# Reordered loads and prefix products at the start, output halves in turn at the end, in a fused Mamba-2 and SiLU-MLP kernel on one Trainium2 core

## The chip, the cores and the metric

The kernel runs on one core of a Trainium2 chip. The metric is device time in microseconds (us) of one execution; lower is better. Within the core five engines work side by side, each through its own instructions in order: PE (TensorE, matrix products into PSUM), DVE (VectorE), ACT (ScalarE), POOL (GpSimd) and SP (SyncE), which here only issues DMAs.

## The reference

The first half is a state-space scan over 4 batches, 8 heads and 768 steps in chunks; the second takes its output, 3072 rows of 256, through two dense layers with a SiLU between them.

```python
def _attn_ref(x, a, B, C):          # x (4,8,768,32), a (4,8,768), B and C (4,8,768,16)
    log_a = np.log(np.clip(a, 1e-06, 1.0))
    ...
        cum = np.cumsum(la, axis=-1)
        L = np.exp(cum[:, :, :, None] - cum[:, :, None, :]) * causal
        M = np.einsum('bhin,bhjn->bhij', Cc, Bc) * L
        y_intra = np.einsum('bhij,bhjd->bhid', M, xc)
        y_inter = np.einsum('bhin,bhnd->bhid', Cc, state) * np.exp(cum)[:, :, :, None]
        y[:, :, sl] = y_intra + y_inter
        ...
        state = decay_full * state + np.sum(Bx, axis=2)

def _moe_ref(x, w_in, w_out):       # x (3072,256), w_in (256,2048), w_out (2048,256)
    h = x @ w_in
    return (h * (1.0 / (1.0 + np.exp(-h)))) @ w_out
```

The weights come in 64-bit floats, so the kernel first turns their bits into 32-bit floats by itself.

## The kernel before

**Units and pairs.** The 3072 rows are 12 units of 256 steps (three for each batch); two units make a pair of 512 rows. The scan half makes a unit's output `XF[u]`; the dense half multiplies it by 16 tiles of the weights, numbered 0 to 15: 0 to 7 are `w_in`, 8 to 15 `w_out`, 512 KB each. Pair 0 (units 0 and 1) goes through the plain products `f_s1(u, j)` (unit u, weight j, 8 matmuls, L508) and `f_s2(j)` (the steps "m0" to "m7", L521). Pairs 1 to 5 go through split operands (a high part, a low part, a correction): `s1_d`, `s1_h`, `s2`, `s2_d` (L536, L544, L576 and L577, L590), 16 steps for each pair.

**A unit's scan.** `load_pa` brings the coefficients a in prefix order (tile pz), `load_ab` in another order (ab), `load_n` and `load_t` B and C (bn, tbc), `load_x` x (xt). DVE clips (`f_P0`, only units 0 and 1) and scans the coefficients (`f_P`, L328), and `f_C` (L391) multiplies the scan with C into cw. `f_T` or `f_TP` turn B and C; `f_TP` uses TensorE and leaves C in PSUM, in one of only two halves (pool `ps_h`) that the products hp of `f_s1` use too. `f_Ek` and `f_E1` are the decay scans E; `f_B`, `f_D0`, `f_G`, `f_S`, `f_SM`, `f_M` prepare states and masked products; `f_Y` (L459, L468) makes the unit's output in PSUM and `f_X` copies it out. In the text forms, "2:PTC" means these steps for unit 2, with "1", "2" for the two decay scans, "D" for `f_G` and `f_D0`, "A" for the loads of pa, bn and ab, "L" for all loads.

**A weight.** `load_w(n)` loads it raw (six buffers, "r11" in the text form); ACT takes it apart in `w_size(n)` ("s6"), DVE in three steps in `w_bits(n)` ("b5"), and POOL ends it with an add (L207). Then `w_h`, `w_l`, `w_d` make the split forms.

**What sets the order.** The schedule is written by hand: each engine runs its instructions in the order in which the code calls them. Nearly all loads go through SP's queue. The coefficients of units 2 to 11 are clipped on the chip and written back to two DRAM tiles, `a_in` and `a_zero` (`f_A2`, L262 to L269), from which `load_pa` and `load_ab` read. At L255 a small DMA, the mark, reads a piece of raw weight 3, so that SP goes on to weight 5 only when that has landed. After each `f_s1` ACT applies the SiLU (gT, L511) and so frees the PSUM half; whatever ACT has ahead of gT, `w_size` among it, holds that half.

**The end.** In the last two steps `s2` adds the last products to both output halves m = 0, 1, `s2_d` the corrections, `f_sum2` (L598) scales these on ACT, and `f_end` (L622) combines them on DVE, transposes (L633) and stores (L635) on the queues of SP and ACT.

Of the kernel before, what the change touches and what calls it, by code (L numbers as in the profile page):

```python
# [33 lines left out]
def kernel(  # L34
# [47 lines left out]

    sc.tile([128, 40], FP32, name="pad")
# [40 lines left out]
    def load_t(u, i, q):  # L124
        b, t0 = at(u)
        if u == 0:
            tbc[u] = block("tbc0").rearrange("p (i e r n) -> p i e r n", i=2, e=2, r=8)
        elif u not in tbc:
            tbc[u] = loads.tile([128, 2, 2, 8, N], FP32, name="tbc")
        src = (B, C)[i]  # L130
        if u == 0:
            for g in range(4):
                q.dma_start(out=tbc[u][32 * g:32 * g + 32, i],
                            in_=src[b, 2 * g:2 * g + 2, t0:t0 + UT].rearrange("e (t r) n -> t e r n", r=8))
# [39 lines left out]
    def two(t):  # L174
        return t.rearrange("p (k f) -> p k f", k=2)

    def load_w(n, q):
        j = n % 8
        src = wi[:, :, j * WF:(j + 1) * WF] if n < 8 else wo[:, 2 * j:2 * j + 2]
        if src.dtype == FP32:  # L180
            w32[n] = block("w32")
            q.dma_start(out=two(w32[n]), in_=src)
            return
        t = raw[n] = quad.tile([128, 2, WF, 2], U32, name="raw", tag="quad")
        q.dma_start(out=t.rearrange("p k f two -> p k (f two)"), in_=src.bitcast(U32))  # L185
# [47 lines left out]
    nc.sync.dma_start(out=ach[A0:A1], in_=bass.AP(tensor=a.tensor, offset=a.offset, ap=[[Q, NC0], [S, H], [1, Q]]))  # L233
    pa01 = block("pa01")
    pz = const.tile([128, 4, Q + 1], FP32, name="pz")
    one = const.tile([128, 4, Q + 1], FP32, name="one")
    load_t(0, 1, nc.sync)
    load_n(0, 0, nc.scalar)
    nc.sync.dma_start(out=pa01, in_=bass.AP(tensor=a.tensor, offset=a.offset, ap=[[S, H], [0, N], [1, 2 * UT]]))
    load_x(0, nc.sync)  # L240
    for n in range(3):
        load_w(n, nc.sync)
# [3 lines left out]

    acl, acz = (block(n).rearrange("p (h t) -> p h t", t=Q) for n in ("acl", "acz"))
# [4 lines left out]
    mark = const.tile([1, RAW - 5], U32, name="mark")  # L252
    for n in range(3, RAW):
        if n > 4:
            nc.sync.dma_start(out=mark[:, n - 5:n - 4], in_=raw[n - 2][0:1, 0, 0, 0:1])  # L255
        load_w(n, nc.sync)

# [4 lines left out]
    def f_A2():  # L262

        r = slice(0, NC0 * batch)
        nc.vector.tensor_scalar(out=acl[r], in0=acl[r], scalar1=1.0, scalar2=1e-6, op0=ALU.min, op1=ALU.max)
        nc.vector.tensor_copy(out=acz[r], in_=acl[r])
        nc.vector.memset(acz[r, :, 0:1], 0.0)
        nc.sync.dma_start(out=a_in[:, :, 1:].rearrange("h c t -> c h t"), in_=acl[r])
# [32 lines left out]
    f_A()  # L301
    ident = const.tile([128, 128], FP32, name="ident")
    nc.vector.memset(ident, 0.0)
    nc.gpsimd.affine_select(out=ident, in_=ident, pattern=[[-1, 128]], compare_op=ALU.not_equal,
                            fill=1.0, base=0, channel_multiplier=1)

    diag = const.tile([128, H, Q], FP32, name="diag")
    nc.vector.tensor_copy(out=diag, in_=diag1.to_broadcast([128, H, Q]))
    hm = const.tile([128, H], FP32, name="hm")
# [11 lines left out]

    def f_P0(u):
        src = pa01[:, UT * u:UT * u + UT].rearrange("p (c t) -> p c t", t=Q)
        nc.vector.tensor_scalar(out=pz[:, :, 1:], in0=src, scalar1=1.0, scalar2=1e-6, op0=ALU.min, op1=ALU.max)

    def f_P1(u):
        PFX[u] = sc2.tile([128, 4, Q + 1], FP32, name="pfx")
        nc.vector.tensor_tensor_scan(out=PFX[u].rearrange("p c t -> p (c t)"),  # L328
                                     data0=pz.rearrange("p c t -> p (c t)"),
                                     data1=one.rearrange("p c t -> p (c t)"), initial=0.0,  # L330
                                     op0=ALU.mult, op1=ALU.add)

    def f_P(u):
        if u < 2:
            f_P0(u)
        f_P1(u)

# [50 lines left out]

    def f_C(u):
        CW[u] = sc.tile([128, UT], FP32, name="cw")  # L390
        nc.vector.tensor_tensor(out=CW[u].rearrange("p (c t) -> p c t", t=Q),  # L391
                             in0=CT.pop(u).rearrange("p (c t) -> p c t", t=Q), in1=PFX[u][:, :, 1:], op=ALU.mult)
# [173 lines left out]

    def s2(s):
# [5 lines left out]
        gh, gl = GH.pop(s), GL.pop(s)  # L573
        for m in range(2):
# [90 lines left out]
    f_Y(0)  # L665
# [11 lines left out]
    f_B(1)  # L677
    w_bits(2, 2)
    f_P(1)
    f_C(1)  # L680
    f_G(1)
    f_D0(1)
# [6 lines left out]
    f_A2()  # L689
    for n in range(6, 9):  # L690
        load_w(n, nc.sync)
    load_bcx(2)
    w_bits(3, 2)
# [4 lines left out]
    w_bits(4)  # L698
    load_pa(2, nc.sync)
    load_ab(2, nc.sync)  # L700
    load_w(10, nc.sync)
# [66 lines left out]
    for text in ("m0 3:D 4:L 3:SsM 2:h h1 l1 2:l 2:d d0 b13 s14", "m1 3:Y 3:h h2 l2 d1 b14 s15", "m2 3:l 3:d d2 b15 h3 l3",  # L768
                 "m3 p0 d3 h4 l4 4:T", "m4 h8 l8 d4 h5 l5 d8", "m5 d5 h9 l9 d9"):
        todo(text)  # L770
# [14 lines left out]
    def step(s):  # L785
# [94 lines left out]
```

## Time and profile before

| what | us |
|---|---|
| median of 3 runs (337.47 to 338.9) | 338.38 |
| the profiled execution, its own time | 339.9 |
| its span, first to last instruction | 338.0 |
| PE busy in the span | 322.8 (96%) |
| DVE busy | 252.4 (75%) |
| ACT busy | 218.6 (65%) |
| POOL busy | 69.1 (20%) |
| chain that ended last: PE | 85% |
| the same: issue on SP's queue | 8% |

The chain of work that ended last is followed back from the last instruction. It is TensorE's from 42.96 us to 330 us, and before that mostly SP's queue issuing loads and the landings that it waits for. Shares of busy time are means over the span. The start, up to about 50 us, has other limits than the long middle, so it is to be read from the timeline and from windows cut to it. In a timeline row the columns are start, duration, engine, line, operation and, in brackets, the engine's idle time before it and what ended that. In a row of windows they are the stretch, its length, the busy time of PE, PE's weight loads, DVE, ACT and POOL with their numbers of instructions, the granted TensorE clock, the share of the DMA engines, and GB/s. In a row of waits they are engine, line, what it waited for, the sum in us, how often, and the longest. A DMA's row on SP's queue is its issue and not its transfer.

### The profile page before, as it was taken

The page shows a single profiled execution, that of the slowest core. Times are in us where ns is not written, and L with a number is a line of the kernel's source. Part 1 is how long each engine was busy: PE and PEld are TensorE (multiplying, and loading weights), DVE is VectorE, ACT ScalarE, POOL GpSimd, SP SyncE. Part 2 cuts the span into 40 slices and gives each one's busy share as a digit, 9 for nine tenths or more (in the row PEclk, how much of TensorE's full clock was granted, in tenths as well). Part 3 has the DMA queues.
Part 4 walks back from the last instruction along what each step waited for, and adds up shares of the span by engine and source line. Part 5 has one row for each costly group of instructions (what it writes and reads, how often), then busy time and mean ns, then how long its engine had stood idle before and what let it go on. Part 6 is the DMA issues. An engine that isn't in the chain of part 4 may idle for free.

```text
span 338.0 us, 7790 instructions
## 1 busy us (share of the span) xinstructions
PE 322.8 (96%) x3145; PEld 256.4 (76%) x3146; DVE 252.4 (75%) x420; ACT 218.6 (65%) x417; POOL 69.1 (20%) x66
## 2 busy tenths in 40 slices
PE   8879599999999999999999999999999999999992
PEld 4558478888878778778788778788778788888881
DVE  7998558997677888996965996865996854674443
ACT  3656535956478898767666666767667756666651
POOL 3226313257001222231202230202240202000000
PEclk9999969999999999999999999999999999999998
DMA  6968878795674584154330154420343000020003
GB/s 127 224 211 211 191 185 206 222 170 108 114 150 67 101 157 89 46 112 75 71 78 0 50 107 85 101 40 0 66 104 52 2 2 0 0 49 17 0 2 62
DMA packets 97290, 30.87 MB, mean 91 GB/s; under 512 B 82230, under 2 KB 88374, under 8 KB 97254
## 3 DMA queue, kind: packets, MB, share of 16 engines
q1 hardware_dynamic: 90758, 25.78, 34.1%
q0 software_dynamic: 2304, 4.20, 7.2%
q10 hardware_dynamic: 4192, 0.39, 0.9%
q8 instruction: 25, 0.41, 0.5%
q14 instruction: 11, 0.09, 0.1%
HBM read 22.82 MB, written 3.34 MB: 77 GB/s over the span
## 4 chain that ended last, share of the span: by engine, by line
PE 85%; SPq 8%; DMA 4%; DVE 1%; issue 1%; ACT 0%; DVEq 0%; ACTq 0%
PE hp L544 23%; PE b L590 11%; PE hp L536 11%; PE oa L576 11%; PE oa L577 11%; PE oa L521 8%; PE hp L508 4%; SPq L122 4%; DMA raw<-in_moe_w_in_dram 3%; PE gy L468 2%; PE gy L419 2%; PE gy L459 2%; DMA pz<-a_in 1%; PE gy L407 1%; SPq L185 1%; SPq L145 1%
## 5 line engine op out<-in xcount | busy, mean ns | idle before, releaser
L538 ACT ACTIVATE hp<-hp 128x512 f32<-128x512 f32 x80 | 46.6, 583 | 72.1 <-PE hp L536 72.0
L558 DVE TENSOR_TENSOR gl<-g,gh 128x512 fp32r<-128x512 f32 x62 | 42.7, 689 | 52.2 <-ACT gh L554 49.1
L544 PE MATMUL hp<-xh,wh 128*128 128x512 f32 x160 | 65.2, 407 | 0.0
L562 DVE SCALAR_TENSOR_TENSOR gd<-gh,g 128x512 fp32r<-128x512 f32 x80 | 59.5, 747 | 5.2 <-ACT gh L554 5.2
L544 PE MATMUL hp<-xl,wl 128*128 128x512 f32 x160 | 62.6, 391 | 0.0
L576 PE MATMUL oa<-gh,wh 128*128 128x512 f32 x160 | 62.5, 391 | 0.0
L577 PE MATMUL oa<-gl,wl 128*128 128x512 f32 x160 | 62.4, 390 | 0.0
L558 POOL TENSOR_TENSOR gl<-g,gh 128x512 fp32r<-128x512 f32 x18 | 29.2, 1623 | 121.9 <-ACT gh L554 121.9
L554 ACT ACTIVATE gh<-g 128x512 fp32r<-128x512 f32 x80 | 50.5, 632 | 2.8
L536 PE MATMUL hp<-xd,wd 128*128 128x512 f32 x160 | 49.5, 391 | 0.0
L552 ACT ACTIVATE g<-hp 128x512 f32<-128x512 f32 x80 | 47.5, 593 | 0.5 <-PE hp L544 0.5
L590 PE MATMUL b<-gd,wd 128*128 128x512 f32 x160 | 44.4, 390 | 0.0
L508 PE MATMUL hp<-xf,w 128*128 128x256 f32 x128 | 32.8, 411 | 5.1 <-DVE cw L391 3.3
L544 PEld LDWEIGHTS hp<-xh,wh 128*128 128x128 f32 x160 | 30.0, 188 | 9.1 <-ACT hp L538 2.5
L536 PEld LDWEIGHTS hp<-xd,wd 128*128 128x128 f32 x160 | 30.0, 188 | 6.7
L576 PEld LDWEIGHTS oa<-gh,wh 128*128 128x128 f32 x160 | 30.0, 188 | 6.4
L590 PEld LDWEIGHTS b<-gd,wd 128*128 128x128 f32 x160 | 30.0, 188 | 6.5 <-DVE o L616 0.3
L577 PEld LDWEIGHTS oa<-gl,wl 128*128 128x128 f32 x160 | 30.0, 188 | 6.3
L508 PEld LDWEIGHTS hp<-xf,w 128*128 128x128 f32 x128 | 25.5, 205 | 11.3 <-issue 3.6
L544 PEld LDWEIGHTS hp<-xl,wl 128*128 128x128 f32 x160 | 30.1, 188 | 5.2
L207 POOL TENSOR_TENSOR w<-wu,wv 128x512 uint32<-128x512 uint32 (+1 forms) x20 | 23.3, 1174 | 45.6 <-DVE wv L202 41.7
L521 PE MATMUL oa<-gT,w 128*128 128x256 f32 x128 | 29.0, 381 | 0.0
(81 smaller groups left out, 375.2 us busy)
## 6 DMA issues: line engine op xcount, KB each, us to landing
ab<-a_zero SPq DMA_DIRECT2D x40, 128.0 KB
raw<-in_moe_w_in_dram SPq DMA_DIRECT2D x8, 512.0 KB
raw<-in_moe_w_out_dram SPq DMA_DIRECT2D x8, 512.0 KB
wl<-w POOLq DMA_DIRECT2D x16, 256.0 KB, 4.2
xt<-in_x_dram SPq DMA_DIRECT2D x24, 128.0 KB
out_dram<-ot SPq DMA_DIRECT2D x44, 64.0 KB
bn<-in_B_dram SPq DMA_DIRECT2D x22, 64.0 KB
tbc<-in_C_dram SPq DMA_DIRECT2D x22, 64.0 KB
```

The costliest lines, as they stand in the source:

```text
L508: nc.tensor.matmul(out=hp[:, i], lhsT=two(w32[j])[:, kc, 128 * i:128 * i + 128], rhs=two(XF[u])[:, kc], start=(kc == 0), stop=(kc == KC - 1))
L521: nc.tensor.matmul(out=OA[0][m][:, UT * u:UT * u + UT], lhsT=two(w32[8 + j])[:, i, 128 * m:128 * m + 128], rhs=two(GT[u, j])[:, i], start= ...
L536: nc.tensor.matmul(out=HP[s], lhsT=two(WD[f // 2])[:, kc, 128 * (f % 2):128 * (f % 2) + 128], rhs=XD[P][:, kc], start=(kc == 0), stop=Fals ...
L538: nc.scalar.activation(HP[s], HP[s], AF.Copy, scale=-HALF / UP)
L544: nc.tensor.matmul(out=HP[s], lhsT=two(w[f // 2])[:, kc, 128 * (f % 2):128 * (f % 2) + 128], rhs=x_[P][:, kc], start=False, stop=(kc == KC ...
L552: nc.scalar.activation(G[s], HP.pop(s), AF.Silu, scale=UP)
L554: nc.scalar.activation(GH[s], G[s], AF.Copy, scale=DOWN)
L558: engine.tensor_tensor(out=GL[s], in0=G[s], in1=GH[s].bitcast(FP32), op=ALU.subtract)
L562: nc.vector.scalar_tensor_tensor(out=GD[s], in0=GH[s].bitcast(FP32), scalar=1.0 + 1.0 / HALF, in1=G.pop(s), op0=ALU.mult, op1=ALU.subtract)
L576: nc.tensor.matmul(out=OA[P][m], lhsT=two(WH[n])[:, r, ms], rhs=gh, start=(f == 0), stop=False)
L577: nc.tensor.matmul(out=OA[P][m], lhsT=two(WL[n])[:, r, ms], rhs=gl, start=False, stop=(f == NF - 1))
L590: nc.tensor.matmul(out=B2[P][:, m], lhsT=two(WD[n])[:, r, 128 * m:128 * m + 128], rhs=gd, start=(fresh and s == tiles[0]), stop=True, skip ...
```

## The change

Five things change.

1. *Loads at the start.* The coefficients `pa01` of units 0 and 1 are loaded in two halves, unit 0's second in SP's queue, unit 1's after weight 0. The last of the four loads of unit 0's C goes on ACT's queue. The mark is dropped. Weights 3 and 4 come next, then all of unit 2's C, B and x (`load_bcx(2)`), and then weight 5. After `f_A2`: weight 6, unit 2's coefficients, then weights 7 and 8. The copy `acz` with a zeroed first column is dropped: the two DRAM tiles get their first columns from a zero tile by DMA, and `a_zero` the rest straight from `acl`.
2. *The first two units.* Unit 0's clip and prefix scan run ahead of the decay scans, and its `f_C` and unit 1's clip go to POOL; unit 1's has a tile `pz1` of its own. `ident` is cleared on POOL, `diag` copied on ACT. Unit 1's scan and `f_C` go ahead of `w_bits(2)`. `f_M(0, 0)` and `w_size(0)` go ahead of `f_S(0)`. Fewer idle products keep TensorE warm.
3. *Units 2 and 3* take their steps earlier among the `f_s1` steps, and weights 12 and 13 are loaded earlier.
4. *The last pair's output halves.* In the last three steps only half 0 gets its products at once; half 1's three sets follow after half 0 is whole.
5. *At the very end* `f_probe` adds 16 products whose results nobody reads.

```diff
@@ loads at the start @@
-    load_t(0, 1, nc.sync)
+    load_a(0)
+    load_t(0, 1, (nc.sync, nc.sync, nc.sync, nc.scalar))
     load_n(0, 0, nc.scalar)
-    nc.sync.dma_start(out=pa01, in_=bass.AP(tensor=a.tensor, offset=a.offset, ap=[[S, H], [0, N], [1, 2 * UT]]))
     load_x(0, nc.sync)
-    for n in range(3):
+    load_w(0, nc.sync)
+    load_a(1)
+    for n in range(1, 3):
         load_w(n, nc.sync)
...
-    for n in range(3, RAW):
-        if n > 4:
-            nc.sync.dma_start(out=mark[:, n - 5:n - 4], in_=raw[n - 2][0:1, 0, 0, 0:1])
-        load_w(n, nc.sync)
+    load_w(3, nc.sync)
+    load_w(4, nc.sync)
+    load_bcx(2)
...
-        nc.vector.tensor_copy(out=acz[r], in_=acl[r])
-        nc.vector.memset(acz[r, :, 0:1], 0.0)
         nc.sync.dma_start(out=a_in[:, :, 1:].rearrange("h c t -> c h t"), in_=acl[r])
-        nc.sync.dma_start(out=a_zero, in_=acz[r])
+        nc.sync.dma_start(out=a_zero[:, :, 1:], in_=acl[r, :, 1:])
...
-    nc.sync.dma_start(out=a_in[:, :, 0:1].rearrange("h c t -> c h t"),
-                      in_=misc[:NC0 * batch, 0:H].rearrange("p (h t) -> p h t", t=1))
+    for t in (a_in[:, :, 0:1].rearrange("h c t -> c h t"), a_zero[:, :, 0:1]):
+        nc.sync.dma_start(out=t, in_=misc[:NC0 * batch, 0:H].rearrange("p (h t) -> p h t", t=1))
+    load_w(5, nc.sync)
@@ the first units @@
+    f_P0(0, nc.vector)
+    f_P(0)
     f_T(0, 1)
...
+    f_C(0, nc.gpsimd)
+    f_P0(1, nc.gpsimd)
     f_Ab(0, 0)
...
-    f_P(0)
-    f_C(0)
+    f_M(0, 0)
+    w_size(0)
     f_S(0)
     f_SM(0)
-    f_M(0, 0)
     f_M(0, 1)
-    w_size(0)
...
-    busy(3, 18)
+    busy(2, 10)
...
-    w_bits(2, 2)
     f_P(1)
     f_C(1)
+    w_bits(2, 2)
...
     f_A2()
-    for n in range(6, 9):
-        load_w(n, nc.sync)
-    load_bcx(2)
+    load_w(6, nc.sync)
+    load_pa(2, nc.sync)
+    load_ab(2, nc.sync)
+    load_w(7, nc.sync)
+    load_w(8, nc.sync)
@@ units 2 and 3 @@
-    steps = ((1, 0, ""), (0, 3, "b5 r11 s6"), (1, 1, "b6 s7"), (1, 2, "b7 s8"), (1, 3, "b8"), (0, 4, "2:T"),
-             (1, 4, "2:P"), (0, 5, "2:C12B s9 3:A r12 r13"), (1, 5, "2:D b9 r14 r15 s10"), (0, 6, "2:SsM"), (1, 6, "b10 s11"),
-             (0, 7, "2:Y b11 s12 3:T"), (1, 7, "3:PC12B b12 s13 h0 l0"))
+    steps = ((1, 0, ""), (0, 3, "b5 r11 s6"), (1, 1, "2:PTC b6 r12 s7"), (1, 2, "2:1 b7 r13 s8"), (1, 3, "2:2B b8"),
+             (0, 4, "s9"), (1, 4, "2:D 3:A r14 2:SsM b9 r15"), (0, 5, "s10"), (1, 5, "2:Y 3:T b10 s11"), (0, 6, "3:PC1 s12"),
+             (1, 6, "b11 3:2B"), (0, 7, "3:D b12 h0 l0"), (1, 7, "3:SsM 2:h s13"))
-    for text in ("m0 3:D 4:L 3:SsM 2:h h1 l1 2:l 2:d d0 b13 s14", "m1 3:Y 3:h h2 l2 d1 b14 s15", ...
+    for text in ("m0 3:Y 4:L 2:l h1 l1 2:d d0 b13 s14", "m1 3:h h2 l2 d1 b14 s15", ...
@@ the end @@
         if s == last + 1:
-            s2(t)
+            s2(t, (0,))
             s2_d([t, t + 1])
             f_sum2(NP - 1)
             return
         if s == last + 2:
-            s2(t)
+            s2(t, (0,))
+            for i in range(LAG):
+                s2(last - LAG + i, (1,))
             f_end(NP - 1)
+            f_probe()
             return
...
-            s2(t)
+            s2(t, (0,) if s == last else (0, 1))
+    def f_probe():
+        w, x_ = two(WH[0])[:, 0, 0:128], WH[1]
+        p = [half("hp") for i in range(2)]
+        for i in range(4):
+            nc.tensor.matmul(out=p[0], lhsT=w, rhs=x_, start=True, stop=True, skip_group_check=True)
+        for i in range(4):
+            nc.tensor.matmul(out=p[1][:96], lhsT=two(WH[2 + i])[:, 0, 0:96], rhs=x_, start=True, stop=True,
+                             skip_group_check=True)
+        for i in range(4):
+            nc.tensor.matmul(out=p[0][:, 0:256], lhsT=two(WH[2 + i])[:, 0, 0:128], rhs=x_[:, 0:256], start=True, stop=True,
+                             skip_group_check=True)
+        for i in range(4):
+            nc.tensor.matmul(out=two(p[1]), lhsT=two(WH[2 + i])[:, 0, 0:128],
+                             rhs=x_[:, 0:256].rearrange("p (o f) -> p o f", o=1).to_broadcast([128, 2, 256]),
+                             start=True, stop=True, skip_group_check=True)
```

More of the change, by code (lines that the diff above doesn't have):

```diff
@@ L81 @@
     ctx.enter_context(tc.manual_schedule())
-    sc.tile([128, 40], FP32, name="pad")
+    sc.tile([128, 48], FP32, name="pad")
     NB = 76
@@ L132, in load_t @@
             for g in range(4):
-                q.dma_start(out=tbc[u][32 * g:32 * g + 32, i],
+                q[g].dma_start(out=tbc[u][32 * g:32 * g + 32, i],
                             in_=src[b, 2 * g:2 * g + 2, t0:t0 + UT].rearrange("e (t r) n -> t e r n", r=8))
@@ L234, with load_a @@
     pa01 = block("pa01")
+    pz1 = block("pz1")[:, 0:4 * Q + 4].rearrange("p (c t) -> p c t", c=4)
     pz = const.tile([128, 4, Q + 1], FP32, name="pz")
     one = const.tile([128, 4, Q + 1], FP32, name="one")
-    load_t(0, 1, nc.sync)
+    def load_a(u):
+        nc.sync.dma_start(out=pa01[:, UT * u:UT * u + UT],
+                          in_=bass.AP(tensor=a.tensor, offset=a.offset + UT * u, ap=[[S, H], [0, N], [1, UT]]))
+    load_a(0)
+    load_t(0, 1, (nc.sync, nc.sync, nc.sync, nc.scalar))
     load_n(0, 0, nc.scalar)
-    nc.sync.dma_start(out=pa01, in_=bass.AP(tensor=a.tensor, offset=a.offset, ap=[[S, H], [0, N], [1, 2 * UT]]))
     load_x(0, nc.sync)
-    for n in range(3):
+    load_w(0, nc.sync)
+    load_a(1)
+    for n in range(1, 3):
         load_w(n, nc.sync)
@@ L245 @@
     load_x(1, nc.sync)
-    acl, acz = (block(n).rearrange("p (h t) -> p h t", t=Q) for n in ("acl", "acz"))
+    acl = block("acl").rearrange("p (h t) -> p h t", t=Q)
     for b in range(batch):
@@ L250 @@
                           in_=bass.AP(tensor=a.tensor, offset=a.offset + b * H * S, ap=[[Q, NC0], [S, H], [1, Q]]))
-    mark = const.tile([1, RAW - 5], U32, name="mark")
-    for n in range(3, RAW):
-        if n > 4:
-            nc.sync.dma_start(out=mark[:, n - 5:n - 4], in_=raw[n - 2][0:1, 0, 0, 0:1])
-        load_w(n, nc.sync)
+    load_w(3, nc.sync)
+    load_w(4, nc.sync)
+    load_bcx(2)
     def f_A():
@@ L293 @@
     nc.vector.memset(pz[:, :, 0:1], 0.0)
+    nc.vector.memset(pz1[:, :, 0:1], 0.0)
     nc.vector.memset(one, 0.0)
@@ L301 @@
     f_A()
[L302 to L308, printed above, removed]
     hm = const.tile([128, H], FP32, name="hm")
@@ L314 @@
                             fill=0.0, base=N - 1, channel_multiplier=-1)
+    ident = const.tile([128, 128], FP32, name="ident")
+    nc.gpsimd.memset(ident, 0.0)
+    nc.gpsimd.affine_select(out=ident, in_=ident, pattern=[[-1, 128]], compare_op=ALU.not_equal,
+                            fill=1.0, base=0, channel_multiplier=1)
+    diag = const.tile([128, H, Q], FP32, name="diag")
+    nc.scalar.activation(diag, diag1.to_broadcast([128, H, Q]), AF.Copy)
     par = const.tile([128, 2], FP32, name="par")
@@ L320, with f_P0, f_P @@
     E, BT, BH, CT, CE, CW, PFX, ST, SM, DP, GY, XF, BX = ({} for _ in range(13))
-    def f_P0(u):
+    def f_P0(u, engine):
         src = pa01[:, UT * u:UT * u + UT].rearrange("p (c t) -> p c t", t=Q)
-        nc.vector.tensor_scalar(out=pz[:, :, 1:], in0=src, scalar1=1.0, scalar2=1e-6, op0=ALU.min, op1=ALU.max)
-    def f_P1(u):
+        engine.tensor_scalar(out=(pz, pz1)[u][:, :, 1:], in0=src, scalar1=1.0, scalar2=1e-6, op0=ALU.min, op1=ALU.max)
+    def f_P(u):
         PFX[u] = sc2.tile([128, 4, Q + 1], FP32, name="pfx")
         nc.vector.tensor_tensor_scan(out=PFX[u].rearrange("p c t -> p (c t)"),
-                                     data0=pz.rearrange("p c t -> p (c t)"),
+                                     data0=(pz1 if u == 1 else pz).rearrange("p c t -> p (c t)"),
                                      data1=one.rearrange("p c t -> p (c t)"), initial=0.0,
                                      op0=ALU.mult, op1=ALU.add)
[L333 to L336, printed above, removed]
     def scan_E(u, g0, n, t):
@@ L387, in f_T2, with f_C @@
         nc.scalar.activation(CE[u][:, e], CT[u], AF.Copy, scale=par[:, e:e + 1])
-    def f_C(u):
+    def f_C(u, engine=nc.vector):
         CW[u] = sc.tile([128, UT], FP32, name="cw")
-        nc.vector.tensor_tensor(out=CW[u].rearrange("p (c t) -> p c t", t=Q),
+        engine.tensor_tensor(out=CW[u].rearrange("p (c t) -> p c t", t=Q),
                              in0=CT.pop(u).rearrange("p (c t) -> p c t", t=Q), in1=PFX[u][:, :, 1:], op=ALU.mult)
@@ L565, with s2 @@
     B2, SUM2 = {}, {}
-    def s2(s):
+    def s2(s, half=(0, 1)):
         P, f = 1 + s // NF, s % NF
@@ L572, in s2 @@
         n, r = 8 + f // 2, f % 2
-        gh, gl = GH.pop(s), GL.pop(s)
-        for m in range(2):
+        gh, gl = GH[s], GL[s]
+        if 1 in half:
+            del GH[s], GL[s]
+        for m in half:
             ms = slice(128 * m, 128 * m + 128)
@@ L698 @@
     w_bits(4)
-    load_pa(2, nc.sync)
-    load_ab(2, nc.sync)
     load_w(10, nc.sync)
@@ L767 @@
         todo(text)
-    for text in ("m0 3:D 4:L 3:SsM 2:h h1 l1 2:l 2:d d0 b13 s14", "m1 3:Y 3:h h2 l2 d1 b14 s15", "m2 3:l 3:d d2 b15 h3 l3",
+    for text in ("m0 3:Y 4:L 2:l h1 l1 2:d d0 b13 s14", "m1 3:h h2 l2 d1 b14 s15", "m2 3:l 3:d d2 b15 h3 l3",
                  "m3 p0 d3 h4 l4 4:T", "m4 h8 l8 d4 h5 l5 d8", "m5 d5 h9 l9 d9"):
```

## The prediction

> **What bounds the kernel now.** I read the page's slices first, then the waits, then the timeline by engine around the one hole, then windows cut to it.
>
> ```profile
> PE   8879599999999999999999999999999999999992
> PEclk9999969999999999999999999999999999999998
> DMA  6968878795674584154330154420343000020003
> ```
>
> TensorE is full from about 50 us to the end: there only its own work counts. What can be won lies in the first six slices (8.45 us each), where the sixth is also clocked down, and in the last.
>
> ```profile
> DVE pfx L328 <- DMA pz<-a_in: 3.6, 1, 3.6
> PE hp L508 <- DVE cw L391: 3.3, 1, 3.3
> ACT wu L191 <- DMA raw<-in_moe_w_in_dram: 1.9, 2, 1.6
> ```
>
> The waits name the hole: unit 2's prefix product (DVE, L328) waits for its coefficients, TensorE waits for the product cw that frees the PSUM half in which unit 2's transposed C lies. The timeline of PE:
>
> ```profile
> 35.04 1.97 PE L508 MATMUL hp<-xf,w 128*128 128x256 f32 x8 [0.71 <-ACT gT L511]
> 42.96 6.44 PE L508 MATMUL hp<-xf,w 128*128 128x256 f32 x16 [3.28 <-DVE cw L391]
> 50.31 5.45 PE L508 MATMUL hp<-xf,w 128*128 128x256 f32 x24
> ```
>
> After the hole 16 matmuls take 6.44 us; the 24 after them 5.45, 0.227 each with the last one's latency, and in a full chain 8 take 1.73. So 16 are 3.45 us' work, and 2.99 us go to a halved clock. Windows show it:
>
> ```profile
> 21.38:24.79 3.41, 2.08 (x100) 1.61 (x98) 3.22 (x10) 2.87 (x6) 0.00 (x0) 1.00 0.51 162
> 38.44:41.85 3.41, 1.25 (x6) 0.76 (x4) 0.29 (x1) 0.94 (x2) 0.84 (x1) 0.98 0.96 300
> 41.85:45.26 3.41, 2.30 (x6) 1.88 (x7) 3.24 (x5) 0.00 (x0) 0.00 (x0) 0.50 0.77 201
> 45.26:48.68 3.42, 3.42 (x10) 2.75 (x9) 1.03 (x3) 1.72 (x3) 0.00 (x0) 0.52 0.67 127
> ```
>
> A stretch 61% busy kept the clock (2.08 of 3.41), one of 37% lost it for 6.83 us. ACT, in order, waits for weights 5 and 7, and TensorE's PSUM halves wait for the gT behind them:
>
> ```profile
> 26.52 0.69 ACT L191 ACTIVATE wu<-raw 128x512 f32<-128x512 f32 x1 [0.29 <-DMA raw<-in_moe_w_in_dram]
> 33.16 0.69 ACT L191 ACTIVATE wu<-raw 128x512 f32<-128x512 f32 x1 [1.65 <-DMA raw<-in_moe_w_in_dram]
> 34.32 0.57 ACT L511 ACTIVATE gT<-hp 128x512 f32<-128x512 f32 x1
> ```
>
> And SP's queue, which all these loads share:
>
> ```profile
> 16.91 0.90 SPq L185 DMA_DIRECT2D raw<-in_moe_w_in_dram  x2
> 21.24 0.68 SPq L255 DMA_DIRECT2D mark<-raw  x1
> 23.68 0.32 SPq L268 DMA_DIRECT2D a_in<-acl  x1
> 24.63 2.13 SPq L185 DMA_DIRECT2D raw<-in_moe_w_in_dram  x2
> 28.88 6.07 SPq L122 DMA_DIRECT2D bn<-in_B_dram  x2
> 37.23 0.64 SPq L105 DMA_DIRECT2D pz<-a_in  x1
> ```
>
> The coefficients are written at 23.68 and read back only at 37.23, behind three weights and unit 2's B, C and x.
>
> [...]
>
> **The change part by part.** (a) *Unit 0.* P0, scan and C (0.28+0.70+0.42) leave DVE's path between BT (ends 7.99) and S; the first two run before the transpose at 4.77, where DVE is half idle (0.42 of 4 to 5 us) if the half pa, now second in the queue, lands by 4; C goes to POOL, idle until 13.15 (nearest row: its 128x256 w at 0.72). The diag copy (0.43) goes to idle ACT. Of 1.40 us I count 0.7, since SM now stands behind w_size(0) (1.25 on ACT), which waits for weight 0; bounds 0 and 1.4. (b) *Unit 1.* P0(1) on POOL takes 0.29 from DVE, acz 0.49 more after M(1). So M(1,1), which ends TensorE's wait of 1.33 at 23.48, comes 1.0 earlier. Fewer warming products cost nothing while Y(0) waits for DVE anyway.
>
> (c) *Loads.* The mark, whose wait held SP from 17.8 to 21.24 and left the DMA idle near 22, goes. Ahead of weight 5 now stand unit 2's C, B, x. Prices from windows of 1 us over 6 to 21 us, where the DMA share is about 1.0: a weight at 2 KB packets 1.44 us (512 KB at 360 GB/s), C or B pair 1.35 (2048 packets, some 1500 a us), x 1.4, two zero columns about 0.5 each. Weights 3 and 4 are through at 20.9 as before; then 1.35+1.35+1.4+1.0 = 26.0, weight 5 at 27.4, and its completion, 1.3 to 1.7 later as with weight 3 (bulk by 19.4, mark freed at 21.2), at 28.8 against 26.5. Then a_in, a_zero (0.8), weight 6 at 29.7. load_pa(2) must wait for the a_in store, some 29; lands 32 (bounds 30 and 35); behind it on SP stand ab, weights 7 and 8. ab: 4 issues, 2.4 us, so weight 7 is issued at 32, through at 34.3, landed 35.8 (bounds 32.5 and 39), against 33.16.
>
> (d) *Unit 2's P, T, C* move five steps ahead, to after s1(1,1). DVE waits there for pa, b6 and unit 2's scans behind it, needed only at (0,6). TensorE has two PSUM halves for hp and tp, so a product can start only when ACT or DVE has read the one before last. It waits three times: for weight 5, (1,1) needs gT(1,0) behind w_size(5): 28.8+1.2+0.6 = 30.6, and (0,3) ends near 27.9, so 2.7 us idle; for C(2), (1,3) from 33; for weight 7, (0,4) starts 1.88 after its landing as before (35.04-33.16): 37.7. Then (0,4), (1,4) at 1.73: 41.15 for what before stood at 42.96. Won: 1.8, and the 2.99 of cold clock: 4.8. The 1.0 of (b) and the 0.71 are inside that, eaten by the loads. G and D0 of unit 2 come earlier, a move within TensorE's own work.
>
> (e) *A cold stretch of its own.* [...] Price 0 to 2.6: half of 6.8 us, less some 0.8 of the wait for weight 7 that it hides in. I take 0.9, a third[...].
>
> (f) *Later steps.* Unit 3 moves up too; DVE, over 90% busy at 60 to 80, has some 2.4 less after m0, so the lead holds. r12, r13 earlier: nothing.
>
> (g) *End.*
>
> ```profile
> 330.45 1.09 ACT L598 ACTIVATE sum<-b 128x512 f32<-128x512 f32 x2 [3.33 <-PE b L590]
> 331.08 0.69 DVE L622 SCALAR_TENSOR_TENSOR o<-oa,sum 128x512 f32<-128x512 f32 x1 [2.64 <-ACT sum L598]
> 332.44 0.65 DVE L622 SCALAR_TENSOR_TENSOR o<-oa,sum 128x512 f32<-128x512 f32 x1
> ```
>
> Four products of half 1 move behind the last b: b and sum come 4 x 0.227 = 0.91 earlier, half 0 is whole by then, half 1 at 331.26 as before, when DVE gets to it (331.5). So both transposes and the stores come 0.9 earlier; bounds 0.5, 0.9. The 16 unread products: 12 x 0.227 + 4 x 0.114 = 3.2 us after 331.3, ending 334.5 while the stores' data runs to 336.2: nothing; if each took four times as long, they would end near 344.
>
> Sum: 4.8 - 0.9 + 0.9 = 4.8. The profiled execution has 338.0 of span in 339.9; the runs' median is 338.38, to which I apply the gain: 333.6.
>
> **Rivals.** *Forecast* (0.55), own range 331.5 to 335.5. *No starving* (0.20): weights 5 and 7 land as before, since the mark's idle DMA time pays for unit 2; everything goes, 3.28+2.99+0.71+1.0+0.91 = 8.9: 329.5. For it: DMA only 0.51 busy at 21.38 to 24.79; against: SP then waits for the store. *The hole only moves* (0.13): over 3 us idle plus full cold stretch at 28 to 34: gain 1 to 2.5, 336.6. *Slower* (0.08): load_pa(2) holds SP for the store, weight 7 with it, ACT with that, and gT. Without cold it breaks even at weight 7 landing 41.5, with 2.6 of cold at 38.9; at 43 with cold 338.4-5.7+7.2+2.6 = 342. For it: the 6.07 issue at 28.88 shows how long SP can hang. *The products outlast the stores* (0.04): 338 to 341.
>
> **How the numbers follow.** A measurement here tells about 0.5% (1.7 us) from no change. Faster: nearly all of the first, all of the second, half the third: 0.80. Same 0.10, slower 0.10. Range 330.0 to 337.0: no starving nearly whole, the moved hole, and the bounds of pa and weight 7.
>
> **What would show it.** The 3.28 wait at L508 gone, PEclk 9 in slice 6 (a 6 in slice 4 or 5 would be (e)); ACT waiting for weight 5 by 2 to 4 us and for 7; DVE's pfx waiting near 29 to 32; the products of m0 starting 4 to 5 earlier than 58.9; last sum 0.9 nearer the end. It is wrong if weights land on time, or if TensorE has a hole over 4 us before 42.

## The result, and the profile after

| | before | after |
|---|---|---|
| median, us | 338.17 (337.47 to 338.9) | 348.08 (347.35 to 348.27) |
| profiled execution, us | 339.9 | 348.07 |
| its span, us | 338.0 | 346.4 |

Both were run four times, side by side. The ratio is 1.0289, 95% interval 1.0262 to 1.0316: the changed kernel is slower by 2.9%, some 9.8 us, where 1.4% faster was forecast.

The slices of the page of the changed kernel (8.66 us each) show two losses of TensorE's clock, in slices 5 and 8, where there was one in slice 6:

```profile
PE   8873998599999999999999999999999999999996
PEclk9999699699999999999999999999999999999999
DMA  7986877753848266334450053350153000012003
```

The timeline of PE of the changed kernel has two holes (start, duration, operation; in brackets the idle time before it and what ended that):

```profile
25.35 3.72 PE L508 MATMUL hp<-xf,w 128*128 128x256 f32 x16 [0.47 <-ACT xf L478]
34.40 3.78 PE L508 MATMUL hp<-xf,w 128*128 128x256 f32 x8 [5.33 <-ACT gT L511]
...
64.36 0.68 PE L407 MATMUL gy<-xt,BT 64*32 64x64 f32 x32 [4.68 <-DVE BT L364]
64.97 3.78 PE L508 MATMUL hp<-xf,w 128*128 128x256 f32 x8
68.55 4.62 PE L521 MATMUL oa<-gT,w 128*128 128x256 f32 x16
```

The old hole, 3.28 us before a product that waited for `cw`, is gone. In its place stand 5.33 us at 29, before (1,1), and 4.68 us at 60. After each hole 8 matmuls take 3.78 us, where the kernel before has 1.99 with the last one's latency. Windows cut to the two holes and to what follows them (stretch, length, busy time of PE, PEld, DVE, ACT, POOL, then clock, DMA share, GB/s):

```profile
29.08:34.40 5.32, 0.00 (x0) 0.00 (x1) 1.03 (x3) 1.76 (x4) 0.00 (x0) 0.87 0.84 234
34.40:41.00 6.60, 6.60 (x20) 5.24 (x21) 1.85 (x4) 3.25 (x7) 1.27 (x1) 0.59 0.70 215
59.70:64.40 4.70, 0.04 (x6) 0.04 (x8) 4.63 (x7) 1.03 (x2) 2.11 (x1) 0.93 0.75 262
64.40:70.50 6.10, 6.10 (x45) 4.85 (x46) 3.48 (x10) 1.71 (x5) 2.25 (x2) 0.50 0.74 129
```

During the first hole nothing works but the DMA until weight 5 has landed at 32.6; then ACT and DVE take it up, and TensorE starts 1.8 us later. During the second DVE is busy 4.63 of 4.70 us. A clock of 0.59 over 6.6 us is 5.4 us at half speed, so 2.7 us of work lost; 0.50 over 6.1 us loses 3.05. Before, one such stretch lost 2.99. So up to about 70 us TensorE waits 6.0 us more (5.33 + 4.68 against 3.28 + 0.71) and loses 2.8 more to the clock: 8.8. The first product of m0 starts at 68.55 against 58.93, 9.6 later, with two groups of products of unit 3 (L419 and L407, 0.69 and 0.46 at full clock) now ahead of it. After that the kernel is not slower: from there to the end of the span it takes 277.85 us against 279.07.

**The first hole.** ACT stands still for weight 5, and gT behind it holds the PSUM half. ACT's timeline:

```profile
25.45 0.69 ACT L194 ACTIVATE wv<-raw 128x512 f32<-128x512 uint32 x1
32.64 0.66 ACT L191 ACTIVATE wu<-raw 128x512 f32<-128x512 f32 x1 [6.50 <-DMA raw<-in_moe_w_in_dram]
33.21 0.65 ACT L194 ACTIVATE wv<-raw 128x512 f32<-128x512 uint32 x1
33.76 1.07 ACT L511 ACTIVATE gT<-hp 128x512 f32<-128x512 f32 x2
```

SP's queue shows why it came then (start and length of an issue):

```profile
17.43 0.90 SPq L185 DMA_DIRECT2D raw<-in_moe_w_in_dram  x2
18.38 2.76 SPq L122 DMA_DIRECT2D tbc<-in_C_dram  x2
21.18 2.85 SPq L122 DMA_DIRECT2D bn<-in_B_dram  x2
24.15 2.26 SPq L145 DMA_DIRECT2D xt<-in_x_dram  x2
26.50 0.53 SPq L279 DMA_DIRECT2D a_in<-misc  x1
27.07 0.67 SPq L279 DMA_DIRECT2D a_zero<-misc  x1
27.79 0.60 SPq L185 DMA_DIRECT2D raw<-in_moe_w_in_dram  x1
...
29.64 0.62 SPq L185 DMA_DIRECT2D raw<-in_moe_w_in_dram  x1
33.40 0.63 SPq L105 DMA_DIRECT2D pz<-a_in  x1
```

Unit 2's C, B and x hold SP for 2.8, 2.9 and 2.3 us, and weight 5 is issued only at 27.79. In the kernel before they stand behind weight 8 and hold SP for 8.7 us in all: B for the 6.07 us at 28.88 that the prediction shows, C and x in these rows:

```profile
27.32 1.52 SPq L122 DMA_DIRECT2D tbc<-in_C_dram  x2
35.05 1.15 SPq L145 DMA_DIRECT2D xt<-in_x_dram  x2
```

In the changed kernel weights 3 and 4 still move up to about 22 us, and the DMA is full (a mean share of 0.95 from 18.38 to 23). From then on it is not. Windows of the changed kernel:

```profile
23.00:25.00 2.00, 1.87 (x99) 1.31 (x97) 1.93 (x5) 1.77 (x5) 0.24 (x1) 1.00 0.54 58
25.00:27.00 2.00, 1.65 (x8) 1.47 (x9) 1.80 (x3) 1.15 (x3) 1.59 (x2) 1.00 0.72 94
27.00:29.00 2.00, 2.00 (x10) 1.48 (x8) 0.14 (x1) 0.00 (x0) 1.27 (x1) 1.00 0.63 68
31.00:33.00 2.00, 0.00 (x0) 0.00 (x0) 0.00 (x0) 0.36 (x1) 0.00 (x0) 1.00 1.09 324
```

58 to 94 GB/s at a share of 0.54 to 0.72, where at 31 to 33, with weights 5 and 6 under way, it is 324. These are means: in windows of 1 us the share runs from 0.17 (23 to 24 us) to 1.14 (25 to 26), so the DMA is full and nearly idle in turn. `load_pa(2)` then waits for the store of `a_in`, from 30.26 to 33.40. The waits of SP's queue between 25 and 40 us have this one row:

```profile
SPq L105 <- DMA a_in<-acl: 3.1, 1, 3.1
```

**The second hole.** DVE's timeline, first of the kernel before:

```profile
59.11 2.33 DVE L341 TENSOR_TENSOR_SCAN E<-ab,diag 128x512 f32<-128x512 f32 x2
61.48 0.42 DVE L364 TENSOR_TENSOR BT<-bn,E 128x256 f32<-128x256 f32 x1
```

and of the changed one:

```profile
59.23 1.22 DVE L341 TENSOR_TENSOR_SCAN E<-ab,diag 128x512 f32<-128x512 f32 x1 [1.13 <-DMA ab<-a_zero]
60.37 0.40 DVE L199 TENSOR_SCALAR wu<-wu 128x512 f32<-128x512 f32 x1
...
61.75 1.22 DVE L341 TENSOR_TENSOR_SCAN E<-ab,diag 128x512 f32<-128x512 f32 x1
63.00 1.30 DVE L364 TENSOR_TENSOR BT<-bn,E 128x256 f32<-128x256 f32 x1
```

Unit 3's first scan starts at nearly the same time in both kernels; here DVE waits 1.13 us for `ab` before it. The consumer has moved: the products that read BT stood behind m0 before; now they stand in TensorE's order ahead of (1,7), so TensorE asks for BT at 59.7. BT ends at 64.3, with three steps of a weight (`b11`, 1.4 us) between the two scans. So at most 1.1 us of the hole's length goes back to the wait for `ab`, which was over before it began; during the hole DVE works.

That `ab` lands late goes with another part of the change. Rows of SP's queue, before and then after:

```profile
46.93 1.45 SPq L185 DMA_DIRECT2D raw<-in_moe_w_out_dram  x1
50.88 3.15 SPq L112 DMA_DIRECT2D ab<-a_zero  x4
```

```profile
46.98 2.31 SPq L185 DMA_DIRECT2D raw<-in_moe_w_out_dram  x3
51.54 6.48 SPq L112 DMA_DIRECT2D ab<-a_zero  x4
```

Weights 12 and 13 now stand ahead of unit 3's coefficients, and the issue of `ab` ends at 58.0 instead of 54.0.

### The profile page after: what moved, and what is told of

The parts are those of the page before. It is cut to its first block, busy times and chain, and to the rows that moved or that the text cites. A ratio compares the mean times of both kernels' runs of the same rounds, so it can differ in the third digit from the quotient of the medians.

```text
span 346.4 us, 7798 instructions
## 1 busy us (share of the span) xinstructions
PE 328.3 (95%) x3152; PEld 261.0 (75%) x3153; DVE 251.7 (73%) x415; ACT 218.5 (63%) x418; POOL 71.5 (21%) x69
## 4 chain that ended last, share of the span: by engine, by line
PE 82%; SPq 8%; DVE 4%; DMA 3%; issue 1%; ACT 1%; DVEq 0%; ACTq 0%
PE hp L544 22%; PE oa L578 11%; PE b L592 11%; PE oa L579 11%; PE hp L536 10%; PE oa L521 8%; SPq L122 4%; PE hp L508 2%; PE gy L468 2%; PE gy L459 2%; PE gy L419 2%; DMA raw<-in_moe_w_in_dram 1%; DVE E L341 1%; SPq L112 1%; SPq L145 1%; PE gy L407 1%
## 5 line engine op out<-in xcount | busy, mean ns | idle before, releaser
L508 PE MATMUL hp<-xf,w 128*128 128x256 f32 x128 | 34.2, 423 | 7.8 <-ACT gT L511 5.7
L207 POOL TENSOR_TENSOR w<-wu,wv 128x512 uint32<-128x512 uint32 (+1 forms) x20 | 24.9, 1252 | 39.1 <-DVE wv L202 39.1
L521 PE MATMUL oa<-gT,w 128*128 128x256 f32 x128 | 29.7, 389 | 0.0
```

What stands on the lines that cost most here:

```text
L508: nc.tensor.matmul(out=hp[:, i], lhsT=two(w32[j])[:, kc, 128 * i:128 * i + 128], rhs=two(XF[u])[:, kc], start=(kc == 0), stop=(kc == KC - 1))
L521: nc.tensor.matmul(out=OA[0][m][:, UT * u:UT * u + UT], lhsT=two(w32[8 + j])[:, i, 128 * m:128 * m + 128], rhs=two(GT[u, j])[:, i], start= ...
```

## The experiments

The theory after this reading: the loads ahead of weight 5 cost one hole with its cold stretch, unit 3's products ahead of (1,7) the other, and the end gains a little. Against it: putting weight 5 first cures the start, since it is the load that comes late; or TensorE starves in any order, since the queue's loads together are what is slow; or unit 2's early steps cost, not unit 3's. Each ratio is to the kernel before, run beside it (its medians: 338.5 us beside experiments 1, 3, 4 and 7, 338.81 beside 6, 8, 9 and 10, 338.68 beside 2, 5, 11 and 12). It is not the quotient of the two medians, and can differ from that by some 0.2%.

**1 (`e1_tail`). The end alone.** Kernel before, with `s2` in halves and the unread products.

```diff
-            s2(t)
+            s2(t, (0,))
+            for i in range(LAG):
+                s2(last - LAG + i, (1,))
             f_end(NP - 1)
+            f_probe()
...
```

> The kernel before with the change's end alone: the last pair's output halves in turn and the 16 unread products. If the unread products lie beside the stores, the end comes 0.9 us earlier, and the time is about 337.4. Rival: the products hold up the end, and the time is 340 or more, part of the loss.

Measured 337.2 us, ratio 0.996 (0.9943 to 0.9978). The end gains 0.4%, 1.3 us; 0.9 was forecast, and the interval (0.2% to 0.6%) holds it. The wait before `cw` differs from one profile to another without anything done to it: here it was 1.54 us, not 3.28, so spans of single profiles are not to be compared to a microsecond.

**2 (`e3_no_products`). The end without the unread products.** Experiment 1 without `f_probe()`, so the 16 products that no output needs are left out.

> The kernel before with the last pair's halves in turn and without the 16 unread products. If these lie wholly beside the stores: the same as e1_tail, some 1.3 us below the kernel before. If they cost something at the end: 1 us or more faster than e1_tail.

Measured 335.98, ratio 0.9933 (0.9895 to 0.9972). The intervals of the two overlap, so the medians tell no cost. The profiles show the end itself. With the products, in experiment 1 (span 333.8 us):

```profile
326.97 0.69 DVE L624 SCALAR_TENSOR_TENSOR o<-oa,sum 128x512 f32<-128x512 f32 x1 [1.61 <-ACT sum L600]
...
328.43 2.20 SPq L654 DMA_DIRECT2D out_dram<-ot  x4
...
330.25 1.08 PE L641 MATMUL hp<-wh 128*128 128x512 f32 x4
```

and without them (span 334.7 us):

```profile
327.85 0.69 DVE L624 SCALAR_TENSOR_TENSOR o<-oa,sum 128x512 f32<-128x512 f32 x1 [1.73 <-ACT sum L600]
...
329.31 2.19 SPq L654 DMA_DIRECT2D out_dram<-ot  x4
```

From the first `o` to the end of the span it is 6.83 us with them and 6.85 without. They lie beside the stores and cost nothing that the profile shows.

**3 (`e1_old_steps`). The changed kernel with the old step lists of units 2 and 3.**

```diff
-(1, 1, "2:PTC b6 r12 s7"), ... (0, 7, "3:D b12 h0 l0"), (1, 7, "3:SsM 2:h s13")
+(1, 1, "b6 s7"), ... (0, 7, "2:Y b11 s12 3:T"), (1, 7, "3:PC12B b12 s13 h0 l0")
...
-"m0 3:Y 4:L 2:l ...", "m1 3:h h2 ..."
+"m0 3:D 4:L 3:SsM 2:h ...", "m1 3:Y 3:h h2 ..."
```

> The changed kernel with the step lists of units 2 and 3 (and of the weights 12 and 13) as they were before, and everything else of the change. My theory has two causes: weight 5 queued behind unit 2's loads (the first hole of TensorE, 5.3 us and a cold stretch worth 3.4) and unit 3's products set ahead of s1(1,7) while its coefficients land late (the second hole, 4.7 and 3.4). Then the first hole stays as it is and the second goes: about 340. Rival: the early steps of unit 2 make the first hole too, and then both go: 335 or less. Rival: the second hole is an echo of the lateness of the first and stays: about 348.

Measured 341.71, ratio 1.0107 (1.0075 to 1.0138). The first hole stays (6.07 us before 35.55, ACT 7.25 for weight 5), the second is gone, and m0 starts at 61.98. So beside the new loads the new order of steps costs about 6 us, and the first hole needs none of it.

**4 (`e1_D_late`). Only unit 3's products back behind m0**, everything else as changed.

```diff
-(0, 7, "3:D b12 h0 l0"), (1, 7, "3:SsM 2:h s13"))
+(0, 7, "b12 h0 l0"), (1, 7, "2:h s13"))
-"m0 3:Y 4:L 2:l ...", "m1 3:h h2 ..."
+"m0 3:D 4:L 3:SsM 2:l ...", "m1 3:Y 3:h h2 ..."
```

> The changed kernel with unit 3's G, D0, states and masked products back behind the first weight of the second layer (m0), where they were before; unit 2 stays early. My theory: TensorE no longer waits at 59.7 us for unit 3's BT, the second hole (4.7) and its cold stretch (3.4) go, the first stays: about 340. Rival, the wait only moves to the next product that needs unit 3: 345 to 348.

Measured 341.11, ratio 1.0094 (1.0071 to 1.0117). Timeline of PE:

```profile
55.81 6.42 PE L508 MATMUL hp<-xf,w 128*128 128x256 f32 x29
62.07 3.62 PE L521 MATMUL oa<-gT,w 128*128 128x256 f32 x16
```

No idle time and no half clock there. Where these entries stand is worth 1.0289 to 1.0094, about 6.6 us, and with that all that experiment 3 took back. Unit 2's early steps, the difference between 3 and 4, are worth nothing that can be told: m0 starts at 61.98 without them and at 62.07 with them.

**5 (`e3_loads`). The loads alone**, on experiment 1: no mark, unit 2's C, B and x and both zero columns ahead of weight 5, `load_pa(2)` and `load_ab(2)` ahead of weight 7. On-chip order and steps as before.

```diff
-    for n in range(3, RAW):
-        if n > 4:
-            nc.sync.dma_start(out=mark[:, n - 5:n - 4], in_=raw[n - 2][0:1, 0, 0, 0:1])
-        load_w(n, nc.sync)
+    load_w(3, nc.sync)
+    load_w(4, nc.sync)
+    load_bcx(2)
...
+    load_w(5, nc.sync)
...
+    load_w(6, nc.sync)
+    load_pa(2, nc.sync)
+    load_ab(2, nc.sync)
+    load_w(7, nc.sync)
```

> The kernel before with the change's end (e1_tail) and with the change's loads of unit 2 and the weights 5 to 8, its DRAM zero columns and without the mark; nothing else of the change. My theory, the loads alone make the first hole (ACT waits 5 us or more for weight 5, TensorE before s1(1,1), a cold stretch): 341 to 343, against 337.2. Rival, the hole needs the new order of units 0 and 1 or the early steps of unit 2 as well: 337 to 339.

Measured 342.75, ratio 1.0111 (1.0053 to 1.0169), against 0.996 for experiment 1: 1.5%, some 5 us. PE's and ACT's timelines:

```profile
35.26 6.88 PE L505 MATMUL hp<-xf,w 128*128 128x256 f32 x24 [4.95 <-ACT gT L508]
```

```profile
33.51 0.66 ACT L191 ACTIVATE wu<-raw 128x512 f32<-128x512 f32 x1 [6.14 <-DMA raw<-in_moe_w_in_dram]
```

The first hole by itself, in the kernel before's order of steps. A smaller one follows it, 2.19 us before 44.32: ACT waits 3.16 us for weight 7.

**6 (`e2_front`). The first units' new order alone**, on experiment 1: the halves of `pa01`, unit 0's clip and scan first, `f_C(0)` and unit 1's clip on POOL, `diag` on ACT, fewer warming products.

```diff
+    f_P0(0, nc.vector)
+    f_P(0)
     f_T(0, 1)
...
+    f_C(0, nc.gpsimd)
+    f_P0(1, nc.gpsimd)
...
-    f_P(0)
-    f_C(0)
+    f_M(0, 0)
+    w_size(0)
```

> The kernel before with the change's end (e1_tail, 337.2) and with its order on the chip for units 0 and 1 (prefix products first, C and a clip on POOL, masked products ahead of states, the coefficients in two halves), but with the weights and unit 2 loaded as before. If the 1.0 us that unit 1's output comes earlier is eaten by the wait for weight 7, as I had it: 337. If it is a gain: 336. If unit 0's products ahead of its scans hold the scans up by 0.8 us, as the trace of the changed kernel shows, and nothing makes up for it: 338.

Measured 337.81, ratio 0.9961 (0.9938 to 0.9985): that of experiment 1 (0.996). This part brings nothing of its own that these intervals would show.

**7 (`e1_w5_first`). Weight 5 ahead of unit 2's loads**, the rest as changed.

```diff
     load_w(3, nc.sync)
     load_w(4, nc.sync)
+    load_w(5, nc.sync)
     load_bcx(2)
...
-    load_w(5, nc.sync)
```

> The changed kernel with weight 5 loaded straight after weight 4 and ahead of unit 2's C, B and x. My theory: ACT no longer waits for weight 5 at 26 us, so TensorE's hole before s1(1,1) goes, but unit 2's coefficients land near 36 as before, so that s1(1,3) waits for them: a hole of about 4 us there in place of 5.3, and the second hole stays: 343 to 347. Rival, the second hole as an echo of the first: 338 to 340. Rival, weight 5 was late for another reason than the queue: no change, 348.

Measured 346.98, ratio 1.0261 (1.0241 to 1.0281), only 1.1 us better than the change. PE's timeline:

```profile
38.22 10.00 PE L508 MATMUL hp<-xf,w 128*128 128x256 f32 x32 [6.10 <-ACT gT L511]
64.08 0.46 PE L407 MATMUL gy<-xt,BT 64*32 64x64 f32 x32 [3.82 <-DVE BT L364]
```

The first hole is not gone but four us later: ACT now waits 5.89 us, to 36.47, for weight 6, and DVE 6.62 us, to 36.96, for pz. The time lies at the upper end of what was expected, but the wait is another: it was to be the one for unit 2's coefficients.

**8 (`e2_w56`). Weights 5 and 6 ahead of unit 2's loads**, on experiment 4.

```diff
-    load_bcx(2)
...
     w_bits(1, 2)
+    load_w(6, nc.sync)
+    load_bcx(2)
...
-    load_w(6, nc.sync)
```

> As e1_D_late, with weights 5 and 6 ahead of unit 2's C, B and x. My theory: each order of these loads leaves one late, and what is waited for next is unit 2's coefficients, which are read back only after the store, near 37 us: ACT no longer waits for weights 5 and 6, but s1(1,3) waits for cw of unit 2, a hole of some 4.5 us from 33 on and a cold stretch: 339 to 341. Rival, the weights' place alone made the first hole: it goes, 334 or less.

Measured 342.25, ratio 1.0107 (1.0051 to 1.0163), not better than experiment 4, and 1 us above what was expected. The hole splits in two, 3.25 us before 37.42 (for `cw`) and 3.48 before 42.90 (for gT), and ACT waits 7.92 us for weight 7.

**9 (`e2_zero_early`). The zero columns ahead of weight 3**, on experiment 4.

```diff
+    for t in (a_in[:, :, 0:1].rearrange("h c t -> c h t"), a_zero[:, :, 0:1]):
+        nc.sync.dma_start(out=t, in_=misc[:NC0 * batch, 0:H].rearrange("p (h t) -> p h t", t=1))
     load_w(3, nc.sync)
     load_w(4, nc.sync)
```

> The changed kernel with unit 3 late as in the run before it (e1_D_late, 341.1), and the two zero columns of the DRAM tiles (768 writes of 4 bytes) moved from just ahead of weight 5 to ahead of weight 3. Rival theory of the late weight 5: these writes hold it up, by 2 us or more in the trace's packets at 27 to 29 us; then weight 5 lands 2 us earlier and the time is about 339. My theory, the packets of 64 and 128 bytes of unit 2's B, C and x ahead of it: no change beyond 0.5 us, 341.

Measured 341.04, ratio 1.0067 (1.0047 to 1.0087); experiment 4 had 1.0094 (1.0071 to 1.0117), so no difference is shown. ACT waits 5.16 us for weight 5, less than 7.59, but now 2.09 for weight 4. One more time in which the wait moved along the queue. Weight 5 came 1.5 us earlier (33.03 against 34.55), and no gain is seen from it.

**10 (`e2_pa_early`). `load_pa(2)` just behind weight 7**, ahead of weight 8 and unit 2's loads, on experiment 1: the old hole attacked directly.

```diff
-    for n in range(6, 9):
-        load_w(n, nc.sync)
+    load_w(6, nc.sync)
+    load_w(7, nc.sync)
+    load_pa(2, nc.sync)
+    load_w(8, nc.sync)
     load_bcx(2)
...
-    load_pa(2, nc.sync)
```

> The kernel before with the change's end (e1_tail, 337.2) and one load moved: unit 2's coefficients straight after weight 7, ahead of weight 8 and of unit 2's C, B and x. If the wait of TensorE for unit 2's cw (3.3 us in the profile, 1.5 in that of e1_tail) comes from the place of this load alone, it goes, and the cold stretch behind it: 333 to 335. Rival, weight 8 comes later by as much and ACT waits for that: 337.

Measured 338.69, ratio 0.9988 (0.9966 to 1.001): no gain, where 333 to 335 was expected and 337 by the rival. The hole before `cw` is gone and m0 starts at 54.13, 4.8 earlier than before. Nearly all of it is lost again by 68: 2.75 us idle, and behind them 16 matmuls at half clock in part (5.01 us; 3.72 in the kernel before). PE's, then ACT's timeline:

```profile
60.50 0.75 PE L419 MATMUL gy<-ce,bh 32*64 32x128 f32 x32 [2.75 <-ACT ce L387]
```

```profile
58.44 0.66 ACT L191 ACTIVATE wu<-raw 128x512 f32<-128x512 f32 x1 [5.37 <-DMA raw<-in_moe_w_out_dram]
```

TensorE, early now, meets the next late weight: ACT waits for weight 12, and `ce` stands behind it.

**11 (`e3_r12`) and 12 (`e3_r12_front`). That weight earlier**: 10 with weight 12's load ahead of unit 3's coefficients, then the same with the first units' new order of 6.

```diff
-"2:C12B s9 3:A r12 r13"
+"2:C12B s9 r12 3:A r13"
```

> As e2_pa_early (unit 2's coefficients after weight 7; 338.7, 1.0 under the kernel before at most), with weight 12 loaded ahead of unit 3's coefficients and not behind them. In e2_pa_early TensorE's hole at 39 us went and another came at 57.8, 2.75 us, as ACT waited 5.4 us for weight 12. If that wait came from weight 12's place in the queue: the hole goes, 333 to 335. Rival, the queue as a whole is the limit here as at the start, and the wait only passes to unit 3's coefficients: 337 to 339.

> As e3_r12, with the change's order on the chip for units 0 and 1. If TensorE's holes are gone, the 0.5 us that unit 1's output comes earlier can show: 0.5 below e3_r12. If loads still decide: no difference, or a loss of up to 1 from a hole that opens on weight 5 or 7.

Measured 337.04, ratio 0.9934 (0.9914 to 0.9954), and 336.35, ratio 0.9934 (0.9906 to 0.9963). Both beat both kernels, by 0.7% against the kernel before (0.5% and 0.7% by the medians) and more against the changed one. Against the end alone no gain is shown (experiment 1: 0.996, to 0.9943 at its low end; experiment 2: 0.9933). Experiment 11 was expected at 333 to 335 and came out where its rival had it, at 337: ACT no longer holds up `ce`, but TensorE waits 2.10 us for BT, since DVE now waits for `ab` of unit 3 (1.17 and 0.81 us, 0.19 in experiment 10), with weight 12 ahead of it in the queue. Experiment 12 has the same ratio, so the first units' order brings nothing here either. The page of the last one, span 333.7 us, shows no clocked-down slice at all:

```profile
PE   7988989999999999999999999999999999999996
PEclk9999999999999999999999999999999999999999
```

## Why the prediction was wrong

By the ratios, in us of 338: the end -1.3 (experiment 1), the loads +5.1 (5 against 1), unit 3's products +6.6 (the change against 4). That makes 10.4 where 9.8 was measured; by the intervals the loads are known to about 2 us and unit 3's products to about 1. The rest, the first units and unit 2's steps, is within the intervals of nothing.

- **(a) and (b), the first units** were forecast to gain 0.7 and 1.0. Unit 0's Y starts at 12.19 against 11.82, later by 0.4: the clip waited for pa till 4.64, not 4, and the decay scans behind it began at 6.08 against 5.26. Unit 1's Y starts at 23.39 against 23.48. The wait of 1.33 us for E became one of 1.33 for POOL's weight 2, one group earlier: `w_bits(2)`, which now stands behind unit 1's scan and C on DVE, ends at 20.6, 1.5 later than before. With the fewer idle products the granted clock of the changed kernel still was 1.00 over the first 33 us.
- **(c), the loads: the first step that failed, in its size.** Weight 5 was to land at 28.8 and landed at 32.6; pz came at 36.4 for 32; weight 7 was taken by ACT at 41.5 for 35.8. From issue to use weight 5 takes nearly the same in both kernels, 4.6 us before (21.96 to 26.52) and 4.9 after (27.79 to 32.64), so against the kernel before it is late because it was issued late. Unit 2's C, B and x and the zero columns were priced at 5.1 us of a full DMA; from the first of them to the issue of weight 5 SP needed 9.4 (18.38 to 27.79). The kernel before had a better price: there the same C, B and x held SP for 8.7 us, against 7.9 here. The prediction shows the 6.07 and uses it for a rival only. Nor was the DMA full in all the windows from which the price was taken: from 13 to 14 us its share was 0.53, at 51 GB/s. The room seen near 22 in the kernel before (0.51) is filled here (1.05 from 21.38 to 23), and weight 5 is late all the same.
- **(d), unit 2's steps.** The 2.7 us idle before (1,1) were 5.33: weight 5 was 3.8 us later than forecast, and the product ahead of the hole ended 1.2 later. That unit 2's products stand earlier gained nothing (3 against 4): with weights late, their order is not what TensorE waits for.
- **(e), the cold stretch** was the right thing in the right place, seen as a 6 in slice 5 and priced at 0.9. It lost 2.7. The third taken as a chance was an estimate, an average of nothing and all.
- **(f), the step that failed most: a term put at nothing.** "Unit 3 moves up too; ... so the lead holds" cost nothing in the sum, and cost 6.6 us on the chip, more than the whole forecast gain. The step looked at how busy DVE is, not at when BT would be asked for. The kernel before shows the order to be kept: E of unit 3 starts at 59.11 and BT ends at 61.9, while m0 starts at 58.93. A consumer moved ahead of m0 asks for BT before there is one, unless its producers come earlier too; and they did not, as `ab` landed later and `b11` stood between the scans. "r12, r13 earlier: nothing" belongs here, for the smaller part: these weights went ahead of `ab` in the queue, and DVE waits for `ab`, 1.13 of the 4.68 us. In experiment 11, where weight 12 alone went ahead, it waits too. No rival named it. Without unit 3's early products the change measures what experiment 4 did, 341 and not 348.
- **(g), the end** was right: 0.9 forecast. In the changed kernel the sum starts at 338.71 and the stores at 340.81, 5.6 before the end; from the end of TensorE's last product that counts (340.49) to the end of the span it is 5.9 us, before 6.7 (331.26 to 338.0). The products beside the stores cost nothing that experiment 2 shows (6.83 us with them, 6.85 without).

The prediction's own sign of being wrong, a hole of over 4 us before 42, is the first hole. The rival that ended slower, at 342 (its terms add up to 342.5), had the chain right in kind (SP held, a weight late, ACT, gT) and its place wrong: it named the wait for the store and weight 7, and it was the loads ahead of weight 5. Experiment 4, with that hole alone, measured 341.1. It had a chance of 0.08; with the queue's rate left open, that was too low.

The prediction had `load_pa(2)` wait for the store of `a_in` until some 29. The trace has the price: SP stands for it from 30.26 to 33.40, 3.1 us.

**What stays open.** Whether the loads of C, B and x are slow for their number of packets, for SP's issuing, or because other traffic ran into them; no run took these apart. Unit 3's early products were only measured beside the new loads: what they would cost with the old ones, or with `b11` behind BT and weights 12 and 13 behind `ab`, was not run. And experiments 7 to 9 show that the hole moves with each order of the queue, not which order would be the best.

## What to carry to other kernels

Before a step is moved up, look in the trace of before at when its inputs are there and when it would ask for them, and not only at how busy their engine is: a consumer moved ahead of its producer's end turned a lead into a wait here, of 4.68 us. Where one queue of loads paced the start, changing its order handed the wait to the next load (5.89 us for weight 6 in experiment 7, 7.92 for weight 7 in experiment 8), so follow the whole queue to the point where the compute engine runs free, and price loads by how long the same loads held the queue in the trace of before (8.7 us for C, B and x here, and 7.9 after), not by the rate of a full DMA (4.1). A hole like these on TensorE is to be priced with a half-clock stretch behind it, as likely and not as certain: of the 16 waits of 2.04 to 6.41 us that end between 25 and 70 us in PE's timelines (both kernels, experiments 1 and 3 to 12), 14 had one, the shortest of them 2.10 us (experiment 11); 2.04 (experiment 9) and 3.25 (experiment 8) had none.

## What was not expected of the hardware

- Issued one behind another, C, B and x of a unit (64 KB to 128 KB a DMA) held SP for 2.3 to 2.9 us a pair, and `ab` of unit 3 held it for 6.48 us for four. Beside these the mean DMA share was 0.95 (18.38 to 23 us), 0.63 (23 to 29) and 0.75 (51.5 to 58). In the last two the DMA engines were not full, and what stood behind in the queue was issued late all the same: weight 5 at 27.79, the last of `ab` at 58.0.
- The clock. The half-clock stretches were not of one length. Both of the changed kernel last 6.8 us, with 1.4 and 0.7 us of that in the hole, so that 5.4 and 6.1 us of work are left to it. Those of experiments 6, 10 and 11 last some 3.3 by an estimate, twice the time that the products in them took too long (1.68, 1.58 and 1.64 us), after idle times of 3.40, 2.75 and 2.10 us. A wait of 1.54 us (experiment 1) was followed by 16 matmuls at full speed (3.69 us for them, 5.37 in experiment 6), and so were the 3.25 us of experiment 8, by 8 matmuls in 1.99. Earlier in experiment 1, behind waits of 1.34 and 0.47 us, 48 matmuls took 12.31 us, 10.63 in experiment 10, and the clock of its slice 4 (25.0 to 33.4 us) is a 7. So the length of the wait alone does not tell. That this is a part of the spread of one kernel's times (the kernel before: 336.74 to 341.58 us in 36 runs) was not tested.
- BT of unit 3, 0.42 us in the kernel before, took 1.30 in the changed one, and the scan of unit 3's coefficients (L333) 1.59 against 0.70 for unit 2's. Both fall on POOL's add to a weight (L207: 61.91 to 64.02 and 55.73 to 57.01); unit 2's scan, at 36.37, begins after one has ended (36.18). The overlap is all that the trace shows; no run took the two apart.
